# Dealing out the matmuls of two neighbouring TensorE operations in turn, in a fused recurrence and long-convolution kernel

## The chip, the cores and the metric

The kernel runs on one core of one Trainium2 chip. The core's engines work side by side, each on its own queue of instructions: TensorE (PE, matmuls; PEld is its loading of weights), VectorE (DVE), ScalarE (ACT), GpSimd (POOL) and SyncE (SP, which here issues the transfers). The metric is the device time of one execution in microseconds. Before the change the median of three runs is 458.21 us (456.58 to 459.52).

## The reference

Two parts follow each other on x of shape 4 x 6272 x 256. First a gated recurrence along the sequence, then a gated long convolution through the Fourier transform:

```python
sig = 1.0 / (1.0 + np.exp(-f_logit))
f = lower_bound + (1.0 - lower_bound) * sig
for t in range(S):                              # S = 6272
    h = f[:, t] * h + (1.0 - f[:, t]) * x[:, t]
    y[:, t] = h

x1, x2, x3 = split(y @ w_proj)                  # three times 256 columns
conv = irfft(rfft(x2, axis=1) * rfft(filter_fft, axis=0), axis=1)
out = (x1 * conv * x3) @ w_out
```

## The kernel before

The four sequences (batches) are worked through one after the other, and the recurrence of the next batch runs beside the convolution of the current one. The sequence length is 6272 = 128 x 49, and the Fourier transform is done as matmuls with small tables in two steps.

The recurrence (`hgrn`) goes in 13 chunks of 512 positions (the last has 128). For each chunk SP loads x and f_logit, ACT takes the sigmoid (L335), POOL multiplies (`u`, L337). Data arrive with positions on the partitions, and the scan needs channels there, so for each half of the channels PE transposes both tensors into PSUM: this is the **transposing operation** `su` (function `turn`, L344 to L350). It makes 16 transposes of 64 x 128 fp32 values (4 in the last chunk): for the gate (from FL), then for x (from XT), for each of four blocks, for the lower and the upper 64 partitions. ACT or DVE then makes the gate factor from one part of the result (`f`, L362 or L364), and DVE scans with it and the other part (L370).

The convolution of a batch has these operations on PE: `P` (L714) projects x2; `F1` (L727) is the first step of the transform; `mini` (L743) and **`F2`, the DFT over q** (function `mm` in `unit`, L784 to L792) the second; DVE multiplies the result by the filter's spectrum (L813), or ACT copies it (L284) and POOL multiplies (L822). `I2` (L832) is the first step back, ACT copies its result into Th (L284), and **`I1`, the inverse DFT over m** (function `inv` in `phase_o`, L886 to L897) the second. DVE multiplies I1's result by the gates (`y`, L901), `proj` (L913) applies w_out, ACT copies the result out and SP stores it. `x13` (L398) makes the gate projections. F2 is 8 matmuls with 64 rows of weights and 256 columns, in pairs for the lower and upper 64 partitions; I1 is 16 matmuls with 64 rows and 128 columns (4 in the last group), in such pairs too. All three kinds use 64 of the 128 rows at a time.

The order of the work is not found by a scheduler at build time. Every piece of work is recorded with `op`, with its predecessors, and the string `ORDER` holds, for each of the 2429 recorded operations, its number, the engine that does it and the first of its PSUM banks (there are eight; su, F2 and I1 take two). `Plan.emit` goes through this string and calls each operation's function, so the instructions of each engine's queue stand in the order of the string. Waits are put in by the framework where an instruction reads what another engine writes, or writes where another still reads, a PSUM bank too.

Of the kernel before, what the change touches and what calls it, by code (L numbers as in the profile page):

```python
# [24 lines left out]
Q = 49  # L25
# [12 lines left out]
UE = 8  # L38
# [18 lines left out]
def m0_of(r):  # L57
    return (128 * q_of(r) - r) // Q


class Plan:

    ROWS = ("su", "F2", "mini", "I1", "FF2", "last")
    ANY = ()
    ENGINES = ("ACT", "DVE", "PE", "POOL", "SP", "MUL")
# [41 lines left out]
    def emit(self):  # L107
        rows, seen = False, set()
        for i, e, b in self.order():
            o = self.ops[i]  # L110
            assert e in o["cost"] and i not in seen and o["preds"] <= seen
# [4 lines left out]
            if e == "PE" and o["kind"] in self.ANY:  # L116
                args.append(rows)
            elif e == "PE":
                rows = o["kind"] in self.ROWS
            o["fn"](*args)  # L120
        assert len(seen) == len(self.ops)
# [51 lines left out]
    "Z7YbxSbzqeTGb1Tb2Qb4Ab3DeJgb6RZrUaCYb0YZ5Yb5YeUOb8BZsEb7Qb9ob+YaBSaFqaGYaDCaEYeWWaKQeXGeeUaMAeYOefEZ+SaNYegMZ/Ca"
    "Oob/QcBAaPYaLYewgeiWe7gaTSeVAcAQcCocDYaXCejGaHUaUYaVqaWYaIEaYYcETcFRcGDe6geBYcHpcIYcJQcLAcKUcOVcPQcMscNYeoAcQNcR"
    "ocTRcVBepYcSYekOaQSaRCeNgaZUaaEcUQcWocXYcYRcaBcZScbqehYccYcdUceMeyAexgciWcjOezYeqQetSfFgfEgeuCevKerAesIcfUcgEchg"
    "ckWclGcsSctKi6Ui8EeZge8AcnWcoOe9Ye0Qe3UfPgfOgcmgcuSe1AcpWe2Ie4Ee5McvCcqGc2Qc3Ie+ScxUfBWfYgcyMfGAfCGfZgc4Qe/CfDOA"
    "uUc5Ac6gfHYfQAfRYfAKi7Ui/Vi9EdAQfIWfJGdBIczSjBFc7QfKOc8Ic0CfLUfjgfSWfigfMEfVScwgc9QfTGfaAfNMfUOdCUfWCfXKelYfbYdF"
    "Wc+AdDEjAQdGOjCAdKSfcUffQdLKdHWfdEfeMcrgfkAflYfgAdMSfhIc1gdIGfmUfpWfnEfoMfqGfrOdUQdVIdNCdPUdQMgCWgDOfwSfxCgAQgBA"
# [16 lines left out]
def kernel(  # L195
# [10 lines left out]
    nc = tc.nc  # L206
# [7 lines left out]
    iden = konst.tile([128, 128], F32, name="iden")  # L214
# [16 lines left out]
    A = HA[:, A0:A0 + AW].rearrange("m (e r k) -> m e r k", r=2, k=64)  # L231
# [17 lines left out]
    FF2 = [("FF2", u) for u in range(NU)] + ["FF2"]  # L249
# [7 lines left out]
    PS = psp.tile([128, 8, 512], F32, name="PS")  # L257
# [61 lines left out]
    def hgrn(b):  # L319
        for c in range(NCHK):  # L320
            t0 = c * CH
            nb = min(CH, S - t0) // 128
            n = nb * 128
            if b == 0:
                k = c % (NX + len(more))
            else:
                k = count["x"] % NX
                count["x"] += 1
            xt, ft = (more[k - NX] if k >= NX else (XT[:, k], FL[:, k]))
            xt, ft = xt[:, 0:nb], ft[:, 0:nb]  # L330
            for dst, src, t in ((ft, f_logit, ("ft", k)), (xt, x, ("xt", k))):
# [6 lines left out]
                xt, xt, ft, op=AOP.mult), r=[("ft", k)], w=[("xt", k)])  # L338
            for kh in range(2):
                cols = slice(kh * 128, kh * 128 + 128)  # L340

                hn = 64 * nb

                def turn(e, pb, ft=ft, xt=xt, cols=cols, nb=nb, hn=hn):  # L344
                    for src, at in ((ft, (0, 768)), (xt, (512 - hn, 512))):
                        for j in range(nb):
                            for p in range(2):
                                ps = slice(64 * p, 64 * p + 64)
                                nc.tensor.transpose(bank(pb)[:, at[p] + j:at[p] + hn:nb],  # L349
                                                    src[ps, j, cols], iden[ps, ps])  # L350
                su = op("su", {"PE": 0.126 * nb}, turn, r=[("ft", k), ("xt", k), "iden"], w=["qT"], take=2)
                j = count["f"] % 2
# [5 lines left out]
                def gate_f(e, pb, fT=fT, hn=hn, kh=kh):  # L358
# [8 lines left out]
                   r=["om"], w=[("fT", j)], src=su)  # L367
# [406 lines left out]
    def unit(b, u):  # L774
# [9 lines left out]
        def mm(e, xb):  # L784
            for o in range(2):
                ks = slice(32 * o, 32 * o + 32)
                for r in range(2):
                    for e2 in range(2):
                        rows = slice(64 * e2, 64 * e2 + 64)
                        nc.tensor.matmul(  # L790
                            PS[:, xb + e2, :].rearrange("p (i k) -> p i k", k=64)[:, :, ks],
                            FT[rows, o, r, :], A[rows, ka:ka + UE, r, ks],  # L792
                            start=(r == 0), stop=(r == 1))
# [88 lines left out]
    def phase_o(b):  # L882
        for g, r0 in enumerate(range(0, Q, 4)):
            rn = min(4, Q - r0)

            def inv(e, cb, r0=r0, rn=rn):  # L886
                tf = late["Th"][:].rearrange("p c b a g -> p (c b a g)")
                for i in range(rn):
                    r = r0 + i
                    sh = (128 - m0_of(r)) % 128  # L890
                    for rr in range(2):
                        c0 = (rr * Q + r) * 128
                        for p in range(2):
                            ps = slice(64 * p, 64 * p + 64)
                            nc.tensor.matmul(PS[:, cb + p, i * 128:(i + 1) * 128],  # L895
                                             tf[ps, c0:c0 + 128], ID[ps, rr, sh:sh + 128],
                                             start=(rr == 0), stop=(rr == 1))  # L897
# [99 lines left out]
```

## Time and profile before

| | |
|---|---|
| median of 3 runs | 458.21 us (456.58 to 459.52) |
| the profiled execution, from first to last instruction | 455.6 us |
| PE busy | 439.6 us, 96%, 6009 matmuls |
| weight loads (PEld) busy | 348.4 us, 76% |
| DVE busy | 407.4 us, 89% |
| ACT busy | 402.3 us, 88% |
| POOL busy | 308.8 us, 68% |
| transposes of su (L349) | 1568 |
| matmuls of F2 (L790), of I1 (L895) | 512, 784 |

Matmuls are pipelined: each is recorded for longer than the distance between two starts, and their ends are modelled, so a busy PE is not a PE at its peak, and the pace of a block of matmuls is read from the starts. Lower and upper halves of a pair start within a few nanoseconds of each other. A line of the timeline merges neighbouring instructions of one kind: start in us from the span's start, length, engine, line, operation, what it writes and reads, shape, count, and in brackets the idle time ahead of it with what ended it. In a group's line, busy time and mean length of one are followed by the idle time of the engine just ahead of such instructions.

### The profile page before, as it was taken

Reading aid. Unit: us, or ns where it says so; the run is one execution under the profiler, and the core shown is the slowest. Engines: PE = TensorE matmul, PEld = TensorE weight load, DVE = VectorE, ACT = ScalarE, POOL = GpSimd, SP = SyncE. Lnnn points to the kernel's source line nnn. Section 1 sums busy time; section 2 is a strip of 40 time slices with the busy share of each in tenths; the row PEclk is TensorE's granted clock in tenths of the full one; section 3 lists DMA queues with packets and bytes.
Section 4 is the critical chain, followed back from the end, with each engine's and each line's share of the span. In section 5 each row is a group of like instructions: output and inputs, shape, how many; then the busy total and the mean of one; then the engine's idle time right before and its main releaser. Section 6 shows DMA issues by size and latency. Waiting matters only on the chain.

```text
span 455.6 us, 14635 instructions
## 1 busy us (share of the span) xinstructions
PE 439.6 (96%) x6009; PEld 348.4 (76%) x6009; DVE 407.4 (89%) x476; ACT 402.3 (88%) x577; POOL 308.8 (68%) x279
## 2 busy tenths in 40 slices
PE   7899999999999999999999999999999999999998
PEld 5687778677767888777668888777778896776797
DVE  8899997799999996999999977999999976989873
ACT  5899999899999987899989998999989858987563
POOL 8888973878899542788995626899994405696400
PEclk9599999999999999999999999999999999999999
DMA  8999999767898985479776896778759721765186
GB/s 326 387 371 345 378 375 361 279 187 233 299 300 282 340 300 237 169 232 374 253 264 219 285 315 272 237 250 303 261 177 317 301 95 46 248 187 185 47 321 246
DMA packets 44434, 120.74 MB, mean 265 GB/s; under 512 B 4304, under 2 KB 7632, under 8 KB 44368
## 3 DMA queue, kind: packets, MB, share of 16 engines
q1 hardware_dynamic: 44368, 119.82, 74.5%
q8 instruction: 47, 0.77, 0.7%
q14 instruction: 19, 0.16, 0.1%
HBM read 86.12 MB, written 31.98 MB: 259 GB/s over the span
## 4 chain that ended last, share of the span: by engine, by line
PE 72%; DVE 11%; ACT 9%; issue 4%; DMA 3%; POOL 1%; SPq 0%; ACTq 0%; DVEq 0%; POOLq 0%
PE PS L398 17%; PE PS L714 9%; PE PS L832 9%; PE PS L913 8%; PE PS L790 7%; DVE HA L370 7%; PE PS L727 6%; PE PS L349 6%; PE PS L895 4%; ACT fTs L362 2%; DMA X<-in_moe_filter_fft_dram 2%; PE PS L600 2%; ACT HA L284 2%; DVE ys L901 1%; ACT X L284 1%
## 5 line engine op out<-in xcount | busy, mean ns | idle before, releaser
L337 POOL TENSOR_TENSOR XT<-XT,FL 128x1024 f32<-128x1024 f32 (+1 forms) x49 | 109.9, 2247 | 55.7 <-ACT FL L335 38.5
L370 DVE TENSOR_TENSOR_SCAN HA<-fTs,HA,PS 128x512 f16<-128x512 f32 (+1 forms) x96 | 112.7, 1202 | 2.0 <-ACT fTs L362 1.1
L398 PE MATMUL PS<-HA,W 128*128 128x490 f16 (+1 forms) x416 | 100.2, 367 | 0.3 <-ACT Th L284 0.2
L822 POOL TENSOR_TENSOR PP<-HA,Hu 98x1008 f16<-98x1008 f16 x42 | 88.0, 2106 | 5.6 <-ACT HA L284 2.6
L284 ACT CAST HA<-PS 128x1024 f16<-128x1024 f32 (+1 forms) x101 | 81.2, 831 | 3.3 <-POOL PP L822 0.8
L901 DVE TENSOR_TENSOR ys<-PS,zt 128x1024 fp32r<-128x1024 f32 (+1 forms) x52 | 58.3, 1151 | 14.0 <-PE PS L895 10.3
L813 DVE TENSOR_TENSOR PP<-PS,Hu 98x1008 f16<-98x1008 f32 x54 | 63.6, 1199 | 1.5 <-PE PS L790 0.7
L362 ACT ACTIVATE fTs<-PS,nomc 128x512 f32<-128x512 f32 (+1 forms) x90 | 59.5, 680 | 4.5 <-PE PS L349 4.2
L398 PEld LDWEIGHTS <-W 128*128 128x128 f16 x416 | 35.3, 97 | 30.2 <-issue 2.9
L428 POOL TENSOR_TENSOR zt<-XS 128x490 f16<-128x490 f32 (+1 forms) x26 | 31.8, 1223 | 39.0 <-DVE ys L901 27.4
L913 PE MATMUL PS<-Wo,ys 128*128 128x256 f32 x392 | 57.5, 293 | 0.4 <-DVE ys L901 0.3
L286 ACT ACTIVATE XS<-PS 128x490 f32<-128x490 f32 (+1 forms) x88 | 51.0, 590 | 6.8 <-DVE zt L419 2.6
L832 PEld LDWEIGHTS <-PP 98*128 98x128 f16 x1024 | 49.2, 98 | 10.1 <-POOL PP L795 1.3
L284 ACT CAST Th<-PS 128x784 f16<-128x784 f32 x63 | 52.0, 828 | 3.4 <-PE PS L832 2.7
L913 PEld LDWEIGHTS PS<-Wo,ys 128*128 128x128 f32 x392 | 49.6, 188 | 4.5 <-DVE ys L901 1.2
L832 PE MATMUL PS<-VA,PP 98*128 98x98 f16 x512 | 52.1, 207 | 0.2 <-POOL PP L795 0.2
L832 PE MATMUL PS<-VB,PP 98*128 98x98 f16 x512 | 51.8, 207 | 0.0
L419 DVE TENSOR_TENSOR zt<-PS,XS 128x490 f16<-128x490 f32 (+1 forms) x78 | 49.2, 648 | 2.7 <-ACT XS L286 0.8
L335 ACT ACTIVATE FL<-FL 128x1024 f32<-128x1024 f32 (+1 forms) x49 | 49.8, 1022 | 0.6 <-DMA FL<-in_f_logit_dram 0.6
L714 PE MATMUL PS<-W,HA 128*128 128x256 f16 x392 | 44.6, 273 | 1.1 <-ACT X L284 1.1
L714 PEld LDWEIGHTS <-HA 128*128 128x128 f16 x392 | 42.9, 142 | 2.0 <-issue 1.3
L349 PE MATMUL PS<-iden,FL 64*128 64x64 f32 x736 | 41.7, 229 | 2.6 <-ACT PP L286 0.6
(119 smaller groups left out, 778.7 us busy)
## 6 DMA issues: line engine op xcount, KB each, us to landing
FL<-in_f_logit_dram SPq DMA_DIRECT2D x45, 512.0 KB, 5.3
XT<-in_x_dram SPq DMA_DIRECT2D x45, 512.0 KB, 6.2
Hu<-H SPq DMA_DIRECT2D x39, 512.0 KB, 4.6
out_dram<-osb SPq DMA_DIRECT2D x24, 512.0 KB, 4.6
out_dram<-PP SPq DMA_DIRECT2D x16, 512.0 KB, 4.8
Hl<-H SPq DMA_DIRECT2D x13, 512.0 KB, 4.7
X<-in_moe_filter_fft_dram SPq DMA_DIRECT2D x9, 512.0 KB, 7.0
out_dram<-HA SPq DMA_DIRECT2D x8, 512.0 KB, 5.7
```

Source lines behind the costliest of these rows:

```text
L284: nc.scalar.copy(dst, src)
L337: op("u", {"POOL": 0.1 + 0.553 * nb}, lambda e, xt=xt, ft=ft: nc.gpsimd.tensor_tensor(xt, xt, ft, op=AOP.mult), r=[("ft", k)], w=[("xt", k)])
L349: nc.tensor.transpose(bank(pb)[:, at[p] + j:at[p] + hn:nb], src[ps, j, cols], iden[ps, ps])
L362: nc.scalar.activation(fT, sT, AF.Identity, scale=by, bias=1.0)
L370: nc.vector.tensor_tensor_scan(h, fT, bank(pb)[:, 512 - hn:512 + hn], init, op0=AOP.mult, op1=AOP.add),
L398: nc.tensor.matmul(PS[:, p, 0:n], W13[:, kh, js], HA[:, HB[kh] + t0:HB[kh] + t0 + n], start=(kh == 0), stop=(kh == 1))
L714: nc.tensor.matmul(pp[:, r - r0, :], column(HB[kh], q_of(r)), W2[:, kh, :], start=(kh == 0), stop=(kh == 1))
L813: nc.vector.tensor_tensor(pr, px.unsqueeze(1).broadcast_to([TB, 2, UE, 63]), hh(), op=AOP.mult)
L822: nc.gpsimd.tensor_tensor(pr, spec[:, o, :, 1:64].unsqueeze(1).broadcast_to([TB, 2, UE, 63]), hh(), op=AOP.mult)
L832: nc.tensor.matmul(PS[:, ib + o, pr * TB:(pr + 1) * TB], PP[:TB, k, o, n, 2 * pr:2 * pr + 2, :], v[:TB], start=(n == 0), stop=(n == 1))
L901: nc.vector.tensor_tensor(late["ys"][:, yk, :, 0:rn * 128], PS[:, cb:cb + 2, 0:rn * 128], late["zt"][:].rearrange("p k r m -> p k (r m)") ...
L913: nc.tensor.matmul(po[:, i, :], late["ys"][:, yk, kh, i * 128:(i + 1) * 128], Wo[:, kh, :], start=(kh == 0), stop=(kh == 1))
```

## The change

Forty times, two operations that stand next to each other in PE's order, one of them su and the other F2 (19 times) or I1 (21 times), are marked in the order string with a new engine name, `JOIN`, on the first of the two. Their functions now give back lists of small pieces instead of issuing everything: a piece is one pair of matmuls for the lower and upper 64 partitions. For a marked pair, `alternate` issues one piece of the first, one of the second, and so on. su gives 8 pieces (2 in the last chunk), I1 gives 8. F2 gives 4 pieces of 256 columns when it stands alone, and in a marked pair 8 pieces of 128 columns, with the weights loaded for each. In the string the second operation of a pair is moved up next to the first, past entries of other engines only; the order of operations on each engine stays as it was, apart from the alternation itself.

```diff
-    ENGINES = ("ACT", "DVE", "PE", "POOL", "SP", "MUL")
+    PIECES = ("su", "F2", "I1")
+    ENGINES = ("ACT", "DVE", "PE", "POOL", "SP", "MUL", "JOIN")
...
+            if e == "JOIN":
+                joined = o["fn"](e, b)
+                continue
             args = [e]
             if o["take"] or o["src"] is not None:
                 args.append(b)
...
+            if joined is not None:
+                assert e == "PE" and o["kind"] in self.PIECES
+                self.alternate(joined, o["fn"]("JOIN", b))
+                joined = None
+            elif o["kind"] in self.PIECES:
+                for piece in o["fn"](*args):
+                    piece()
+            else:
+                o["fn"](*args)
...
+    def alternate(a, b):
+
+        for k in range(max(len(a), len(b))):
+            for pieces in (a, b):
+                if k < len(pieces):
+                    pieces[k]()
...
-                    for src, at in ((ft, (0, 768)), (xt, (512 - hn, 512))):
-                        for j in range(nb):
-                            for p in range(2):
-                                ps = slice(64 * p, 64 * p + 64)
-                                nc.tensor.transpose(bank(pb)[:, at[p] + j:at[p] + hn:nb],
-                                                    src[ps, j, cols], iden[ps, ps])
+                    def piece(src, at, j):
+                        for p in range(2):
+                            ps = slice(64 * p, 64 * p + 64)
+                            nc.tensor.transpose(bank(pb)[:, at[p] + j:at[p] + hn:nb],
+                                                src[ps, j, cols], iden[ps, ps])
+                    return [lambda src=src, at=at, j=j: piece(src, at, j)
+                            for src, at in ((ft, (0, 768)), (xt, (512 - hn, 512))) for j in range(nb)]
...
+            n = UE // 2 if e == "JOIN" else UE
+
+            def piece(o, i, r):
                 ks = slice(32 * o, 32 * o + 32)
-                for r in range(2):
-                    for e2 in range(2):
-                        rows = slice(64 * e2, 64 * e2 + 64)
-                        nc.tensor.matmul(
-                            PS[:, xb + e2, :].rearrange("p (i k) -> p i k", k=64)[:, :, ks],
-                            FT[rows, o, r, :], A[rows, ka:ka + UE, r, ks],
-                            start=(r == 0), stop=(r == 1))
+                for e2 in range(2):
+                    rows = slice(64 * e2, 64 * e2 + 64)
+                    nc.tensor.matmul(
+                        PS[:, xb + e2, :].rearrange("p (i k) -> p i k", k=64)[:, i:i + n, ks],
+                        FT[rows, o, r, :], A[rows, ka + i:ka + i + n, r, ks],
+                        start=(r == 0), stop=(r == 1))
+            return [lambda o=o, i=i, r=r: piece(o, i, r)
+                    for o in range(2) for i in range(0, UE, n) for r in range(2)]
...
+                return [lambda i=i, rr=rr: piece(i, rr) for i in range(rn) for rr in range(2)]
```

More of the change, by code (lines that the diff above doesn't have):

```diff
@@ L61 @@
 class Plan:
-    ROWS = ("su", "F2", "mini", "I1", "FF2", "last")
-    ANY = ()
-    ENGINES = ("ACT", "DVE", "PE", "POOL", "SP", "MUL")
+    PIECES = ("su", "F2", "I1")
+    ENGINES = ("ACT", "DVE", "PE", "POOL", "SP", "MUL", "JOIN")
     def __init__(self):
@@ L107, in emit @@
     def emit(self):
-        rows, seen = False, set()
+        seen, joined = set(), None
         for i, e, b in self.order():
             o = self.ops[i]
-            assert e in o["cost"] and i not in seen and o["preds"] <= seen
+            assert e in o["cost"] or e == "JOIN" and "PE" in o["cost"]
+            assert i not in seen and o["preds"] <= seen
             seen.add(i)
+            if e == "JOIN":
+                joined = o["fn"](e, b)
+                continue
             args = [e]
@@ L115, in emit @@
                 args.append(b)
[L116 to L121, printed above, removed]
+            if joined is not None:
[7 more added lines that the diff above has]
+                o["fn"](*args)
+        assert len(seen) == len(self.ops) and joined is None
+    @staticmethod
+    def alternate(a, b):
[3 more added lines that the diff above has]
+                    pieces[k]()
 ORDER = (
@@ L144 @@
-    "dgJQqNeANogK3XK4SK0BK1GNpgK2YK5HK6qJVUJRYK7YNfYJXENUQNVAK8WNWIK+GNYTNygNzgMrgNZDK9SK/CLAYLBXLCWJJQNaLLGSJZsLDHLE"
+    "H8YH6YHuEIHSIICIFWIGGH9oH+YKTYKUUKWMKVVKZQKXFKYYH2SH3CKbIIUgIJWIM0MkQIKOIOsINYIQEIRYMlAIdgIVSImgIZCMmIH/WIXqIAGI"
+    "YYIWYIPYMoUMpEMqMNEgKaTKcDIvQIwAIaYISWIfYI5gKJYIeyMwQIgKIhYITGIiqIjYIbUMxAMyIKeSIcEKdYNFgKgCM02InUM1GIzSIrsIsYIp"
+    "EIqYNQgIoYJCgI0CIkQIlAM2OKfUKjVKkSKlFKhsNGANHYI6QKmqKnYI8oI+oI/YI9YNRgIxWIyGI1UItSI2EM8WJLgMngIuCI3UI4MI7YJDwNAS"
+    "JFoM9GJGYNcgJEYJHAJIYM+ONBCJAUKoRKpQNSANTYKqBNCKNIWJBENJGKroKsYKtRKvBJNYNM0JMSNNENKOJOCNOMJUgKuQKyRKzWJPYKwoKxYN"
@@ L145 @@
+    "dgJQqNeANogK3XK4SK0BK1GNpgK2YK5HK6qJV0NUQJRYK7YNfYJXENVAK8WNWIK+GNYTNygNzgMrgNZDK9SK/CLAYLBXLCWJJQNaLLGSJZsLDHLE"
     "uLFYNqALIKJKAJaYJSTJTDLHXNgQNkVN8gNhANlFLJvLKYNbgNiILLUNrYLMSLQTLNEJYYLRXLOqNmNLSDLVUKiYLTHN9gLXEM/gJWYNsQNtALWS"
-    "NvTLYqLZYN0ANwDLUYLaVLPYNuINxLJbWJcGOHgN1YLbSR8QR9RLfWLcFNnYLdqLeYLgOR+AR/BN+ALkULlMN2SN/YOGgN3CN4KN5QNXYOQgN6AN"
-    "7ILhWLiGLmUNDALuSLvKNPYLpWLnELqOOIAOAQOBAOCILjgORgODUObgOagOJYLwSOEELxCLrWLsGLtgOFML4QL5ILogOKSOSANLgLzWONUOlgOk"
-    "gL0OOOEOLCL6QL7AL1WL9QL8gL2GOcAMzAOPMOTYOMKL+IMCUOUWOXSOYCMDMVAgOZKU/gL/QOVGOWOMAAOdYMEUMFEMHSMIKOeQOfAOgIOhUVLg"
@@ L149 @@
-    "OiEM3YVMgOjMOmASBWSCXSEHSDGMJSMKCOnYOoQOpIOrWOsGOqIMBgNjAOtOVXgLygMMUMRSVYgVNAMNMMSKL3gVBAO2QPAWO8UO3IMLgO9EPBGM"
+    "NvTLYqLZYN0ANwDLUYLaVLPYNuINxLJbWJcGOHgN1YLbSR8QR9RLfWLcFNnYLdqLeYLgOR+AR/BN+ALk0N2SLlMN/YOGgN3CN4KN5QNXYOQgN6AN"
+    "7ILhWLiGLmUNDALuSLvKNPYLp2OAQLnELqOOIAOBAOCILjgORgODUObgOagOJYLwSOEELxCLrWLsGLtgOFML4wOKSL5ILogOSANLgLz2ONUOlgOk"
+    "gL0OOOEOLCL6QL7AL1WL9QL8gL2GOcAMzAOPMOTYOMKL+IMC0OUWOXSOYCMDMVAgOZKU/gL/QOVGOWOMAAOdYMEUMFEMHyOeQMIKOfAOgIOhUVLg"
+    "OiEM3YVMgOjMOmASBWSCXSEHSDGMJSMKCOnYOoQOpIOr2MMUOsGOqIMBgNjAOtOVXgLygMRSVYgVNAMNMMSKL3gVBAO2QPAWO8UO3IMLgO9EPBGM"
@@ L152 @@
     "SQVSRQQFgPksPnYSOpQOgPlYSSFSToPfYPgSPhCPjYPvYP0UP1ESVXSXHPsuPtYQXgP2QP3IPoSPpCP9UQBsPrYP4WSUYP5GVOYSWQSaRScBP/sQ"
-    "qgQAYPwSP6WP7OQHYP+YQCYPxCSbRSdBSYoQGUQIEQJYSeYQKsQzgVDSVECQgQQhAVFKQLYQDWQQYQEGQPUQRsQYQQaAQTsQUYQ8gQkSQlCQMWQc"
+    "qgQAYPwSP6WP7OQHYP+YQCYPxCSbRSdBSYoQG0VDSQIEQJYSeYQKsQzgVECQgQQhAVFKQLYQDWQQYQEGQPUQRsQYQQaAQTsQUYQ8gQkSQlCQMWQc"
     "oQbYRFgQdYQZYSfQQNGSgUQiSQSYShAQjCSkVQmWMagQnGSmNQVQQWAQrSSisSjYVHUVjgQtqQoWQpOQvCQwYSZYVkgSlQSnoSpRQeSVIEVJMQuY"
-    "SrBQfCQsYQ0WQ4GQ2uQ3YQ5YRYgVPQVQAVTSVwgVvgRhgQxUVRIVUCVVKQ1YSqXSuWQyESsHStYRQUQ+YSwGRSQRREQ9WQ/uRBuRGSRTARKCQ6UR"
+    "SrBQfCQsYQ02VPQQ4GQ2uQ3YQ5YRYgVQAVTSVwgVvgRhgQxUVRIVUCVVKQ1YSqXSuWQyESsHStYRQUQ+YSwGRSQRREQ9WQ/uRBuRGSRTARKCQ6UR"
@@ L156 @@
     "HYROQRCYQ7ERIqSoYVGYRPARLYRJYSvWSzTS1DSxuRAYRqgRDUS0XS2vVlAVmYS3YMdQMeAMfgRZSRbqRdqRcYRUWVbQREES4SSPYSyYVKgRVGRW"
-    "URXMRaYVcAVxAVdIRMWRjYRNGS5TS7DVfUV7gV8gRrWVnQS6CVyYS8YReYRvGVWYRzgVgMVoAVhMVpIVrSWHgWIgRtGS9XS+UVegVqgS/HTAsVsC"
-    "VtKRfVRsYRgFRwYTCXTDQTHRTIWTEHTFoTGYTJBTKuRiURuYRksV9AVzSV0CRmEV3QWSgWRgV1KTMWTLYTOGRnYV+YTNXTPvTRUTTETSVTUtTWWV"
-    "4AV5IRxSTQYTXXTbURyCTcVTgSTYGThTTdETZvWJAWKYTetTiKRlYRoQR1YTjrTkYRpAR0UR4ER2sV/WR3YWDQWbgWcgTBYWAGWBOWEATlSTmTTn"
+    "URXMRaYVcAVxAVdIRMWRjYRNGS5TS7DVf0RrWV7gV8gVnQS6CVyYS8YReYRvGVWYRzgVgMVoAVhMVpIVrSWHgWIgRtGS9XS+UVegVqgS/HTAsVsC"
@@ L160 @@
+    "VtKRfVRsYRgFRwYTCXTDQTHRTIWTEHTFoTGYTJBTKuRi0VzSRuYRksV9AV0CRmEV3QWSgWRgV1KTMWTLYTOGRnYV+YTNXTPvTRUTTETSVTUtTWWV"
+    "4AV5IRxSTQYTXXTbURyCTcVTgSTYGThTTdETZvWJAWKYTetTiKRlYRoQR1YTjrTkYRpAR00V/WR4ER2sR3YWDQWbgWcgTBYWAGWBOWEATlSTmTTn"
     "CTorTpYTfYR5YTqUTsETrVTttTvSTwUWLWTuYTxCWFITyETzYR6SWMGWNOR7CT0UT1VT2ET3tTVYTaYT5QT6RT7AT8pT9YT+SabQSKYWTAT4YT/K"
-    "adAWUYUDUUEMWOWViYWlgUIQWPGWQOUASUJIWmgWdAUBCUCgUFUUGEUNWUOOWeYWVSWYQWvgWWCWXKUKUWZAWfWWaIULEWwgUSSUTKWiUW5gWgGW"
-    "6gUPQWhOWnAWjEWkMUQAUHgUUSUVCWxAUXWUYOUcQUdIWoYWpUWqEWrMWsSXDgXEgWtCWuKWyYW7AW8YUZWAgQUaGUhQUiIWzUW2WV2AWCYW3GW4"
@@ L163 @@
-    "OUMgdfgW0EW1MUeSUfCUjQUmWUnOUkAW9SW+CW/KXAQXBAXCIXFAXGYacUagVaiFUbgV6AdqgaeEdegUoWXHSXICXJKXKUd2gXLEXMMVSAUrQUsI"
+    "adAWUYUD0WOWUEMViYWlgUIQWPGWQOUASUJIWmgWdAUBCUCgUFUUGEUN2WVSUOOWeYWYQWvgWWCWXKUKUWZAWf2USSWaIULEWwgUTKWiUW5gWgGW"
+    "6gUPQWhOWnAWjEWkMUQAUHgUUSUVCWxAUXWUYOUcQUdIWoYWpUWqEWrMWsSXDgXEgWtCWuKWyYW7AW8YUZWAgQUaGUhwWzUUiIW2WV2AWCYW3GW4"
+    "OUMgdfgW0EW1MUeSUfCUjQUm2W9SUnOUkAW+CW/KXAQXBAXCIXFAXGYacUagVaiFUbgV6AdqgaeEdegUoWXHSXICXJKXK0UrQd2gXLEXMMVSAUsI"
     "d3gUpGUwSUxKVuYWGYXTUXlWXmGXUMXNQURgXOAXXWUWgXYGXVSd4AXfQXgAXRUXSMUtWUqgUuOXhQdgAXiIXWCXPUXQMXZSd5YdsAdrgdhYXjWX"
@@ L165 @@
     "aCXbQXkGXdSXcAUggXeCU6UU1WU2OUyQU7MUzAUvgafYXnSXpWXqGXrUUlgXsEU0gahQalRanBXoKajoXtSXuCXxWXzuakYX0YX1uamQaqRaoAas"
-    "BdtYU3UXvSU4EX2YU5gapYXwKX6YXyYX5QX9oX+YdiWYRSarUatsavVX7AX8YX3QYCYYbgdjGdkOYSCaxFYBSYFqX4AYDCdmUeCgeDgYEYdnEdoM"
+    "BdtYU3UXvSU4EX2YU5gapYXwKX6YXyYX5wdiWX9oX+YYRSarUatsavVX7AX8YX3QYCYYbgdjGdkOYSCaxFYBydmUYFqX4AYDCeCgeDgYEYdnEdoM"
     "auYYJWawQYLGX/RYMYYKYYNuYOYa0Ta2LYkgYABa1Wa3Ga4YYTUYGYayoYVRduWYUEdvOa5TazYY2gYWBa7DYXUdwOYYEa6QYtga8Aa+RbAJdlYa"
-    "9YYHSYICYZUYaMYdYYcWYgGYhYYeuYlQYpAYPSYqYYmYdxYa/UYfYYQCbDRYnoYoYbEVYuSeEAYwCbFJdyWdzGd6QbGtePgbISbBsbHYbJUbNVYy"
+    "9YYHSYICYZUYaMYdYYcWYgGYhYYeuYlQYpAYPSYqYYmYdxYa/UYfYYQCbDRYnoYoYbEVYuydyWeEAYwCbFJdzGd6QbGtePgbISbBsbHYbJUbNVYy"
@@ L173 @@
[L173 to L177, printed above, removed]
@@ L178 @@
-    "Wc+AdDEjAQdGOjCAdKSfcUffQdLKdHWfdEfeMcrgfkAflYfgAdMSfhIc1gdIGfmUfpWfnEfoMfqGfrOdUQdVIdNCdPUdQMgCWgDOfwSfxCgAQgBA"
+    "EZnoaSgZoYZxSZyCZqYeKWemgeLGbCYbnRbrQbppbqYbtIbsUeRYecAZiSZmYblYbwVbyFeMOengZjCAlQbusedYZ4weSWbvYZ8oZ9YZ1UZ2MZ6A"
+    "Z7YbxSbzqeTGb1Tb2Qb4Ab3DeJgb6RZrUaCYb0YZ5Yb5YeUOb8BZsEb7Qb9ob+YaByeWWaFqaGYaDCaEYaKweeUeXGaMAeYOefEZ+SaNYegMZ/Ca"
+    "Oob/QcBAaPYaLYewgei2aTSe7geVAcAQcCocDYaXCejGaHUaUYaVqaWYaIEaYYcETcFRcGDe6geBYcHpcIYcJQcLAcKUcOVcPQcMscNYeoAcQNcR"
+    "ocTRcVBepYcSYekOaQSaRCeNgaZUaaEcUQcWocXYcYRcaBcZScbqehYccYcdUceMeyAexgci2eqQcjOezYetSfFgfEgeuCevKerAesIcfUcgEchg"
@@ L179 @@
+    "ckWclGcsSctKi6Ui8EeZge8Acn2e0QcoOe9Ye3UfPgfOgcmgcuSe1AcpWe2Ie4Ee5McvCcqGc2we+Sc3Icx0fBWfYgcyMfGAfCGfZgc4Qe/CfDOA"
+    "uUc5Ac6gfHYfQAfRYfAKi7Ui/Vi9EdAwfIWfJGdBIczSjBFc7wfLUfKOc8Ic0CfjgfSWfigfMEfVScwgc9QfTGfaAfNMfUOdCUfWCfXKelYfbYdF"
+    "Wc+AdDEjAQdGOjCAdKyfcUffQdLKdHWfdEfeMcrgfkAflYfgAdMSfhIc1gdIGfmUfp2dUQfnEfoMfqGfrOdVIdNCdPUdQMgCWgDOfwSfxCgAQgBA"
     "f2Uf3Mf0Sf1Kf8Qf9IfsUftEf6Wf7GfuSfvCf4Qf5IfyUfzEgESgFCf+Wf/GdRQc/gdSAdZSdaKgGUgHEdJggKWgLOgISgJCgMQgNAjDYgQUi+Yj"
@@ L887, in inv, with piece @@
                 tf = late["Th"][:].rearrange("p c b a g -> p (c b a g)")
[L888 to L897, printed above, removed]
+                def piece(i, rr):
+                    sh = (128 - m0_of(r0 + i)) % 128
+                    c0 = (rr * Q + r0 + i) * 128
+                    for p in range(2):
+                        ps = slice(64 * p, 64 * p + 64)
+                        nc.tensor.matmul(PS[:, cb + p, i * 128:(i + 1) * 128],
+                                         tf[ps, c0:c0 + 128], ID[ps, rr, sh:sh + 128],
+                                         start=(rr == 0), stop=(rr == 1))
+                return [lambda i=i, rr=rr: piece(i, rr) for i in range(rn) for rr in range(2)]
             i1 = op("I1", {"PE": 0.115 * rn}, inv, r=[("Th", u) for u in range(NU)] + ["ID"], take=2)
```

8 lines of the change are left out of this document (1 added, 7 removed).

## The prediction

> **What bounds the kernel now.** First the page: engine shares (busy us, share, instructions) and the chain that ended last.
>
> ```profile
> span 455.6 us, 14635 instructions
> ...
> PE 439.6 (96%) x6009; PEld 348.4 (76%) x6009; DVE 407.4 (89%) x476; ACT 402.3 (88%) x577; POOL 308.8 (68%) x279
> ...
> PE 72%; DVE 11%; ACT 9%; issue 4%; DMA 3%; POOL 1%; SPq 0%; ACTq 0%; DVEq 0%; POOLq 0%
> PE PS L398 17%; PE PS L714 9%; PE PS L832 9%; PE PS L913 8%; PE PS L790 7%; DVE HA L370 7%; PE PS L727 6%; PE PS L349 6%; PE PS L895 4%; ACT fTs L362 2%; DMA X<-in_moe_filter_fft_dram 2%; PE PS L600 2%; ACT HA L284 2%; DVE ys L901 1%; ACT X L284 1%
> ```
>
> TensorE (PE) holds 72% of the chain, DVE and ACT together 20%. The lines of the change, L349 (transposes), L790 (DFT) and L895 (inverse DFT), are 17% of it. Next come busy times by stretch; all 40 joined pairs lie between 107.9 and 365.0 us.
>
> ```profile
> core 0: us, PE busy (x) PEld busy (x) DVE busy (x) ACT busy (x) POOL busy (x), PEclk, DMA share, GB/s
> 107.90:365.00 257.10, 251.90 (x3790) 199.39 (x3792) 241.50 (x262) 240.42 (x349) 188.28 (x142) 1.00 0.78 271
> 285.00:335.00 50.00, 50.00 (x743) 36.40 (x742) 48.91 (x61) 48.79 (x76) 47.87 (x41) 1.00 0.76 261
> ```
>
> PE idles 257.1 - 251.9 = 5.2 us there. In 285 to 335 us PE, DVE and ACT are full at once: a delay on any of the three has little to hide behind. The clock is 1.00 throughout, so it plays no part.
>
> **The change, part by part.** In before, an operation's matmuls stand in one block: 16 transposes (8 pieces of two, one for each half of the rows), then 16 inverse-DFT matmuls (8 pieces) or 8 DFT matmuls of 256 columns. After, 40 neighbouring blocks a and b are dealt out a, b, a, b. In the listing of the built program DVE, ACT, POOL and SP keep their order and instructions, no queue is passed and no DMA moves; PE keeps the order of its operations. Of the pairs 21 hold an inverse DFT and 19 a DFT; each of these 19 is split into 16 matmuls of 128 columns, so PE gets 19 x 8 = 152 more matmuls and as many weight loads. Three pairs hold a short transposing operation of 2 pieces, so there are 37 x 8 + 3 x 2 = 302 transposing pieces.
>
> *PE's own work.* Durations of one, by shape:
>
> ```profile
> L398 PE MATMUL PS<-HA,W 128*128 128x490 f16 x384 | 94.1, 370 | 0.3 <-ACT Th L284 0.2
> L349 PE MATMUL PS<-iden,XT 64*128 64x64 f32 x736 | 39.6, 223 | 0.6 <-POOL XT L337 0.6
> L790 PE MATMUL PS<-HA,FT 64*128 64x256 f16 x512 | 37.9, 271 | 0.2
> L895 PE MATMUL PS<-ID,Th 64*128 64x128 f16 x784 | 28.7, 216 | 1.0 <-DVE HA L370 0.5 <-ACT X L284 0.3 <-ACT PP L286 0.2
> L349 PEld LDWEIGHTS PS<-iden,FL 64*128 64x128 f32 x736 | 32.1, 138 | 13.7 <-DVE HA L370 2.6 <-ACT afs L284 1.3 <-ACT PP L286 1.3
> L895 PEld LDWEIGHTS <-Th 64*128 64x128 f16 x784 | 23.6, 94 | 7.6 <-issue 3.5 <-ACT Th L284 0.9 <-ACT XS L286 0.3
> ```
>
> These overlap, so the pace is read from starts. The timeline of a pair with an inverse DFT and of one with a DFT, both without a wait between a and b (start, length, engine, line, count):
>
> ```profile
> 240.69 0.37 PE L398 MATMUL PS<-HA,W 128*128 128x490 f16 x1
> 240.99 0.62 PE L895 MATMUL PS<-ID,Th 64*128 64x128 f16 x16
> 241.45 0.41 PE L349 MATMUL PS<-iden,FL 64*128 64x64 f32 x8
> 241.71 0.42 PE L349 MATMUL PS<-iden,XT 64*128 64x64 f32 x8
> 241.96 0.61 PE L895 MATMUL PS<-ID,Th 64*128 64x128 f16 x16
> ...
> 299.48 0.61 PE L790 MATMUL PS<-HA,FT 64*128 64x256 f16 x8
> 299.93 0.41 PE L349 MATMUL PS<-iden,FL 64*128 64x64 f32 x8
> 300.17 0.41 PE L349 MATMUL PS<-iden,XT 64*128 64x64 f32 x8
> 300.42 0.35 PE L349 MATMUL PS<-iden,FL 64*128 64x64 f32 x6
> ```
>
> Inverse DFT: 241.45 - 240.99 = 0.46 us for 8 pieces, 57 ns each. Transposes: 0.25 us for 4 pieces, 62 ns each, and it stays 0.25 (241.71 to 241.96) when the next thing is no transpose but an inverse DFT, whose load is short (94 against 138 ns). So a transposing piece holds its place for about 62 ns whoever follows: the time lies in the matmul itself, or at least as much there as in the load. Its 223 ns say the same: columns cost (370 - 216)/(490 - 128) = 0.43 ns each, 64 of them would make 189, and 223 are 34 more. The other seam, inverse DFT to transpose, stands inside the 0.46: a full 57. Dealt out, a pair of pieces then takes 57 + 62 as before. A DFT block is 0.45 us for 4 pieces of 256 columns, or 8 halves of 56: nothing again. I take **0** for PE's work (bounds: -35 ns for each transposing piece if its excess over 64 x 0.43 = 27 ns could hide, which is rival B; and a price for switching, rival C).
>
> The Trainium skill's TensorE: Matmul & The Clock Gate, section Weight-path perf modes, has loads of 128 weights fast unless they are FP32, and its section What happens when you issue a matmul has a load pulled ahead under a running matmul. By these and its N/2.4 + 2.5 ns a transposing piece would take an estimated 29 ns once its load hides, and the change would save about 10 us of PE work; the 0.25 us seam speaks against it.
>
> *Waits of b, now inside a.* This is the cost I expect. An operation writes two PSUM banks and waits at its first matmul until their last reader is done. PE takes the matmuls in the program's order, so after the change b's first piece, second in the row, holds back 7/8 of a.
>
> ```profile
> 121.87 0.89 ACT L284 CAST Th<-PS 128x784 f16<-128x784 f32 x1
> ...
> 122.20 0.72 PE L790 MATMUL PS<-HA,FT 64*128 64x256 f16 x8
> ...
> 122.82 0.46 PE L349 MATMUL PS<-iden,FL 64*128 64x64 f32 x8
> 123.07 1.20 DVE L813 TENSOR_TENSOR PP<-PS,Hu 98x1008 f16<-98x1008 f32 x1
> 123.11 0.42 PE L349 MATMUL PS<-iden,XT 64*128 64x64 f32 x8
> 123.16 0.67 ACT L284 CAST HA<-PS 98x512 f16<-98x512 f32 x1
> ```
>
> ACT's Th copy frees b's banks at 121.87 + 0.89 = 122.76. In before the DFT block fills that time, and the transposes start at 122.82 having lost 0.06 us. After, PE does one DFT piece at 122.20, then stands from 122.26 to 122.81: 0.55 us idle, and the pair ends 0.49 us later than now. I read all 40 pairs so (start of a, end of the last reader of b's banks, remaining pieces at the paces above; where the x half of the transposes comes late, L337 at half way). First and last:
>
> ```profile
> 107.39 0.66 DVE L291 TENSOR_SCALAR XS<-PS 128x490 f32<-128x490 f32 x1
> 107.91 0.77 PE L790 MATMUL PS<-HA,FT 64*128 64x256 f16 x8
> ...
> 364.39 0.28 PE L349 MATMUL PS<-iden,FL 64*128 64x64 f32 x2
> 364.89 0.80 PE L895 MATMUL PS<-ID,Th 64*128 64x128 f16 x18 [0.16 <-DVE HA L370]
> ```
>
> The first frees at 108.05 and loses 0.12 us, the last loses 0.11. Nine of the 40 lose nothing (240.99 is one), the worst 0.59; together **7.7 us** of new PE idle time.
>
> *Consumers of a.* a's last piece comes just ahead of b's last, so whoever reads a is released later by b's length (about 0.45 us) plus the stall: over the 40 pairs 27.6 us, 19.9 of it beyond the PE delay itself. In the fence above DVE L813 (123.07) and ACT L284 (123.16) take the DFT's result at once; released 1.1 us later, ACT has only L362 of the transposes next, which ends up late too. Waits of this kind exist already:
>
> ```profile
> DVE ys L901 <- PE PS L895: 10.3, 8, 2.7
> ACT fTs L362 <- PE PS L349: 4.2, 11, 1.3
> ```
>
> (total us, times, longest). b's consumers gain nothing: b does not end sooner.
>
> *Sum.* How much reaches the end? I weigh by the chain's shares: PE delay 7.7 x 0.72 = 5.5; consumers' delay 19.9 x 0.20 = 4.0; together 9.5, of which I take 9, as the nine pairs without a stall show that slack exists. Bounds: 0 (the 5.2 us of PE idle time and unread slack take all) and 27.6 (all of it lands). The profiled span is 455.6; the median of the runs lies 2.6 above. 458.2 + 9 = **467 us**.
>
> **Rivals.**
>
> *A, slack takes it.* Engines that come late at one pair catch up before the next; pairs are 257/40 = 6.4 us apart and the mean delay is 0.7. For it: POOL and DMA work is unaffected, and 5.2 us of PE idle time is there. Against: the full stretch 285 to 335, with 8 pairs in it. It gives 0 to 4 us: 458 to 462.5.
>
> *B, the transposes' loads hide (the side that is not slower).* If 35 of the 62 ns are the FP32 load, and the DFT's matmul covers it, PE saves 302 x 35 ns = 10.6 us. Place: between a DFT piece and the next transposing piece, where loads could run 57 ns ahead. For it: the 138 against 94 ns of load. Against: the 0.25 us seam. Net: 467 - 10.6 x 0.72 = 459.4. It decides from 9/0.72/302 = 41 ns a piece: above that the kernel is not slower than before. If stalls are slight too (A and B), about 451.
>
> *C, switching costs.* Going from 128-row to 64-row matmuls costs now: 240.69 to 240.99 is 0.30 us where 490 columns at 0.43 take 0.21. Should a transpose and a DFT matmul (both 64-row) charge a tenth of these 90 ns at each of some 14 new switches, 40 x 14 x 9 ns x 0.72 = 3.6 us more: 471; with a fifth, 474 and beyond. Against: neither seam at 241.45 nor at 241.96 shows any.
>
> **How the numbers follow.** Forecast 0.55 (463 to 473); A 0.15; B 0.20, of which 0.08 ends below 453.6; C 0.10. The measurement tells about 1% (4.6 us) from no change. Faster by over 1%: 0.08. Within: A and the rest of B, 0.27. Slower: 0.65. Low end 456 takes in A and most of B; the high end is 7.7 whole plus 0.4 of 19.9, so 15.7 on 458.2: 474.
>
> **What would show it.** In the profile after: L349, L790 and L895 interleave in the 40 places; starts of successive pieces stay 57 and 62 ns apart (B: they shrink to about 57 + 30; C: they grow). In the place that is now 122.20, PE idles some 0.5 us between the first DFT piece and the first transposes, ended by ACT L284. PE idle time before L349 and L895 grows by some 5 to 8 us in sum, the waits of ACT L284, DVE L813 and L901 for L790 and L895 grow by several us, and PE's share of the span falls. PE matmuls count 6161. Wrong I am if the pace inside pairs shrinks well below 119 ns for two pieces, or if idle time grows but the span doesn't.

## The result, and the profile after

The changed kernel takes 470.97 us (median of 4 runs, 469.57 to 472.74), the kernel before 457.4 us in the same comparison: ratio 1.0293, 95% interval 1.0257 to 1.0329, or 11.8 to 15.0 us slower. The forecast was 467 us (456 to 474), so the direction was right, and the loss of 13.4 us is half again as large as the 9 expected.

In the listing of the changed kernel lines have moved: the transposes stand on L363 (before L349), the DFT on L807 (L790), the inverse DFT on L913 (L895), ACT's copies on L299 (L284), its gate factor on L378 (L362), DVE's scan on L386 (L370), its product with the spectrum on L832 (L813). From the page of the changed kernel, engine shares and the chain that ended last:

```profile
span 469.0 us, 14940 instructions
...
PE 443.0 (94%) x6161; PEld 350.1 (75%) x6161; DVE 409.9 (87%) x476; ACT 404.1 (86%) x577; POOL 308.7 (66%) x279
...
PE 64%; ACT 13%; DVE 13%; issue 5%; DMA 3%; POOL 1%; SPq 0%; ACTq 0%; DVEq 0%; POOLq 0%
```

The engines do the same work (DVE 409.9 against 407.4 us, ACT 404.1 against 402.3; PE 443.0 against 439.6 with 152 more matmuls, whose recorded times overlap), and each of them has a smaller share of a longer span: they wait more. The chain's share on PE fell from 72 to 64%, that on ACT and DVE rose from 20 to 26%. By stretch, the one with the pairs:

```profile
core 0: us, PE busy (x) PEld busy (x) DVE busy (x) ACT busy (x) POOL busy (x), PEclk, DMA share, GB/s
108.00:376.00 268.00, 255.34 (x3941) 201.23 (x3939) 243.01 (x262) 241.31 (x347) 188.10 (x142) 1.00 0.76 261
295.00:345.00 50.00, 48.29 (x783) 35.98 (x782) 45.83 (x58) 45.93 (x70) 45.32 (x39) 1.00 0.72 241
```

PE now idles 268.0 - 255.3 = 12.7 us there (5.2 before). The stretch in which PE, DVE and ACT were all full (50.00, 48.91 and 48.79 of 50 us) has holes on all three. The pace of the matmuls is unchanged. This is the timeline of a pair without a wait, which alternates all the way:

```profile
360.98 0.22 PE L913 MATMUL PS<-ID,Th 64*128 64x128 f16 x2
361.04 0.23 PE L363 MATMUL PS<-iden,FL 64*128 64x64 f32 x2
361.10 0.22 PE L913 MATMUL PS<-ID,Th 64*128 64x128 f16 x2
361.15 0.23 PE L363 MATMUL PS<-iden,FL 64*128 64x64 f32 x2
361.22 0.22 PE L913 MATMUL PS<-ID,Th 64*128 64x128 f16 x2
361.27 0.23 PE L363 MATMUL PS<-iden,FL 64*128 64x64 f32 x2
361.33 0.22 PE L913 MATMUL PS<-ID,Th 64*128 64x128 f16 x2
```

From one inverse DFT piece to the next are 361.33 - 360.98 = 0.35 us for three of each kind: 117 ns for two pieces, where blocks took 57 + 62 = 119. A pair with a DFT, from 240.72 to 241.43 us in this trace, gives 0.71 us for six of each kind, 118 ns. And this is the place whose counterpart in before the prediction showed at 122.20, all engines:

```profile
124.68 0.87 ACT L299 CAST Th<-PS 128x784 f16<-128x784 f32 x1
...
124.99 0.29 PE L807 MATMUL PS<-HA,FT 64*128 64x128 f16 x2
...
125.61 0.28 PE L363 MATMUL PS<-iden,FL 64*128 64x64 f32 x2 [0.33 <-ACT Th L299]
...
126.49 0.23 PE L363 MATMUL PS<-iden,XT 64*128 64x64 f32 x2
...
126.74 1.21 DVE L832 TENSOR_TENSOR PP<-PS,Hu 98x1008 f16<-98x1008 f32 x1 [0.81 <-POOL PP L814]
126.77 0.58 ACT L299 CAST HA<-PS 98x512 f16<-98x512 f32 x1 [0.62 <-ACT fTs L378]
```

One DFT piece starts at 124.99; the first transposes stand until ACT's Th copy is done (124.68 + 0.87 = 125.55) and start at 125.61. So PE starts nothing for 0.55 us, as worked out; the pair takes 0.39 us longer than in before, where 0.49 was worked out. The two readers of the DFT start 1.75 and 1.78 us after it (126.74, 126.77), where it was 0.87 and 0.96 (123.07 and 123.16 after 122.20), and both engines stand idle for it, 0.81 and 0.62 us. The brackets name POOL and ACT, but in the trace the queues of DVE and ACT stand on a wait for PE until 126.70 and 126.74; POOL (126.08 + 0.53 = 126.61) and ACT's L378 (126.15) were done before. The two costs of the forecast are both to be seen here.

### The profile page after: what moved, and what is told of

It is laid out like the page before. It is cut to its first block, busy times and chain, and to the rows that moved or that the text cites. A ratio compares the mean times of both kernels' runs of the same rounds, so it can differ in the third digit from the quotient of the medians.

```text
span 469.0 us, 14940 instructions
## 1 busy us (share of the span) xinstructions
PE 443.0 (94%) x6161; PEld 350.1 (75%) x6161; DVE 409.9 (87%) x476; ACT 404.1 (86%) x577; POOL 308.7 (66%) x279
## 4 chain that ended last, share of the span: by engine, by line
PE 64%; ACT 13%; DVE 13%; issue 5%; DMA 3%; POOL 1%; SPq 0%; ACTq 0%; DVEq 0%; POOLq 0%
PE PS L414 15%; PE PS L730 9%; PE PS L932 8%; PE PS L851 7%; PE PS L363 7%; DVE HA L386 6%; PE PS L807 6%; PE PS L743 6%; PE PS L913 3%; ACT fTs L378 3%; DVE ys L920 3%; ACT HA L299 2%; DMA X<-in_moe_filter_fft_dram 2%; ACT Th L299 2%; PE PS L671 2%
## 5 line engine op out<-in xcount | busy, mean ns | idle before, releaser
L386 DVE TENSOR_TENSOR_SCAN HA<-fTs,HA,PS 128x512 f16<-128x512 f32 (+1 forms) x96 | 112.7, 1201 | 4.2 <-ACT fTs L378 3.4
L299 ACT CAST HA<-PS 128x1024 f16<-128x1024 f32 (+1 forms) x101 | 80.6, 824 | 9.0 <-PE PS L363 3.2
L832 DVE TENSOR_TENSOR PP<-PS,Hu 98x1008 f16<-98x1008 f32 x54 | 63.7, 1199 | 5.9 <-PE PS L363 1.6
L378 ACT ACTIVATE fTs<-PS,nomc 128x512 f32<-128x512 f32 (+1 forms) x90 | 58.4, 668 | 8.7 <-PE PS L363 6.2
L363 PE MATMUL PS<-iden,FL 64*128 64x64 f32 x736 | 49.8, 231 | 7.0 <-DVE HA L386 2.1
L299 ACT CAST Th<-PS 128x784 f16<-128x784 f32 x63 | 51.8, 827 | 3.9 <-PE PS L851 3.0
L363 PEld LDWEIGHTS PS<-iden,FL 64*128 64x128 f32 x736 | 38.0, 138 | 19.6 <-DVE HA L386 4.7
L807 PE MATMUL PS<-HA,FT 64*128 64x256 f16 (+1 forms) x664 | 47.6, 246 | 1.4 <-ACT Th L299 0.9
```

The source lines that it names most:

```text
L299: nc.scalar.copy(dst, src)
L363: nc.tensor.transpose(bank(pb)[:, at[p] + j:at[p] + hn:nb], src[ps, j, cols], iden[ps, ps])
L378: nc.scalar.activation(fT, sT, AF.Identity, scale=by, bias=1.0)
L386: nc.vector.tensor_tensor_scan(h, fT, bank(pb)[:, 512 - hn:512 + hn], init, op0=AOP.mult, op1=AOP.add),
L807: nc.tensor.matmul(PS[:, xb + e2, :].rearrange("p (i k) -> p i k", k=64)[:, i:i + n, ks], FT[rows, o, r, :], A[rows, ka + i:ka + i + n, r, ...
L832: nc.vector.tensor_tensor(pr, px.unsqueeze(1).broadcast_to([TB, 2, UE, 63]), hh(), op=AOP.mult)
```

## The experiments

Theory: (1) b's wait for its PSUM banks now stands in the middle of a, and PE idles; (2) a's readers are released late; PE's own work is the same. Rivals: the extra matmuls or the switching between kinds cost time, so that every pair costs alike; or one of (1) and (2) is the whole of it. All edits below are against the changed kernel. Added lines shown alone stand in place of the four lines that the first edit takes out of `alternate`, but for the run in which b starts after half of a, which keeps them; `first` and `kind` are the kinds of a and of b, handed over as a third argument. Differences are against the kernel before, run on the same chip, and worked out as (ratio - 1) x 457.4 to 458.1 us. The ratio on record is not the quotient of the two medians and differs from it by up to 0.3%: in the first run below the median is 457.34 us and that of before 457.74. A delay is said to land as far as it lengthens the whole kernel. The lateness of a is how much longer than in before a takes from its first to its last matmul; it delays a's readers. All latenesses below are sums over the pairs.

**Halves without alternation.**

```diff
-        for k in range(max(len(a), len(b))):
-            for pieces in (a, b):
-                if k < len(pieces):
-                    pieces[k]()
+        for piece in a + b:
+            piece()
```

> The 40 pairs stay in blocks, one operation after the other; only the 19 DFTs of the pairs are cut into halves of 128 columns. Theory (the loss is b's wait standing inside a, and a's readers released late): no loss, 0 to +0.5 us against before (19 x 8 more matmuls at 2 to 3 ns). Rival 'more PE work' (the 152 extra matmuls and loads cost): +3 us or more of the 13.4.

Measured: 457.34 us, ratio 1.0017 (0.9993 to 1.0041), +0.8 us (-0.3 to +1.9). The 152 extra matmuls are not where the 13.4 us are. All runs below have these halves in the pairs that they keep marked, as the changed kernel has.

**Eleven pairs, and the other 29.**

```diff
+    FREE = (844, 760, 755, 775, 1140, 1283, 1293, 1582, 1674, 1831, 1856)
...
+            if e == "JOIN" and i not in self.FREE:
+                e = "PE"
             if e == "JOIN":
```

> Only the 11 pairs alternate in which b's banks were free before a's second piece in the trace of before; the other 29 run as in before. Theory: hardly a wait is added, only 11 x 0.44 us of later release of a's readers, of which a fifth lands: about +1 us. Rival 'every alternating pair costs alike' (switching, or late readers landing whole): 11/40 of 13.4 = +3.7 us.

With `i in self.FREE` the other 29 alternate:

> Only the other 29 pairs alternate, those in which b had to wait for its banks. Theory: nearly all of the loss, +11 to +13 us. Rival 'every pair costs alike': 29/40 of 13.4 = +9.7 us.

Measured: eleven pairs 459.45 us, ratio 1.0047 (1.002 to 1.0074), +2.2 us (0.9 to 3.4); the 29 others 470.64 us, ratio 1.0263 (1.0225 to 1.0302), +12.0 us (10.3 to 13.8). Alike per pair would be 3.7 and 9.7, outside both intervals. The loss is 0.20 us for each of the eleven and 0.41 for each of the others, which have the waits; but the lateness of a is larger there too, 0.78 us a pair against 0.47, so this run does not tell the two apart. And 2.2 is twice what I gave the eleven, a first sign, within the interval, that late readers were priced too low.

**The wait alone.** b's first piece stands second, then a is finished, then b:

```diff
-        for k in range(max(len(a), len(b))):
-            for pieces in (a, b):
-                if k < len(pieces):
-                    pieces[k]()
+        for piece in a[:1] + b[:1] + a[1:] + b[1:]:
+            piece()
```

> All 40 pairs, but dealt out only once: first piece of a, first piece of b, then the rest of a as a block, then the rest of b. b's wait for its banks stands in the same place as in after, but a is finished one block earlier (0.4 us) than in after. Theory by the forecast's weights: the PE waits remain, 7.7 to 8.8 us of pair time, and with what they delay +8 to +10 us. Rival 'late readers are the main loss': +4 us or less.

**The late reader alone.** Only a's last piece is put off:

```diff
+        for piece in a[:-1] + b[:-1] + a[-1:] + b[-1:]:
+            piece()
```

> All 40 pairs, blocks as in before, but the last piece of a is put off until just before the last piece of b. b's wait stands behind seven pieces of a as in before, so PE waits no longer; a's readers are released 0.4 us late, 40 x 0.43 = 17 us in sum. Theory by the forecast's weights: a fifth lands, +2 to +4 us. Rival 'late readers are the main loss': +9 us or more.

Measured: wait alone 463.35 us, ratio 1.0137 (1.0102 to 1.0173), +6.3 us (4.7 to 7.9); late reader alone 465.51 us, ratio 1.0182 (1.0149 to 1.0215), +8.3 us (6.8 to 9.8). Neither reading of what the main loss is holds by itself. The first came out below the 8 to 10 us that I expected, the second at more than double. The sum, 14.6, is the 13.4 of the whole within the intervals, but the two runs do not split it cleanly: the wait holds a back as well, so the lateness of a is 13.5 us with the wait alone, 23.0 with the late reader alone, and 28.6 in the changed kernel, less than the two together.

Where does the late reader cost? The same place in the run with late readers alone (its listing is two lines shorter: transposes L361, DFT L805, scan L384):

```profile
123.62 0.62 PE L805 MATMUL PS<-HA,FT 64*128 64x128 f16 x14
...
124.24 0.46 PE L361 MATMUL PS<-iden,FL 64*128 64x64 f32 x8
124.54 0.35 PE L361 MATMUL PS<-iden,XT 64*128 64x64 f32 x6
...
124.73 0.22 PE L805 MATMUL PS<-HA,FT 64*128 64x128 f16 x2
...
125.04 1.21 DVE L830 TENSOR_TENSOR PP<-PS,Hu 98x1008 f16<-98x1008 f32 x1 [0.47 <-issue]
125.06 0.58 ACT L297 CAST HA<-PS 98x512 f16<-98x512 f32 x1 [0.28 <-ACT fTs L376]
```

PE goes from the 14 DFT matmuls to the transposes as in before (0.62 us from start to start, 0.62 there: 122.20 to 122.82), yet the readers start 1.42 and 1.44 us after the DFT began instead of 0.87 and 0.96, and DVE idles 0.47, ACT 0.28 us. They are full engines (in 107.9 to 135 us of before DVE is busy for 26.3 and ACT for 26.85 of 27.1 us), and PE later waits for what they free: here are idle times ahead of the transposes and their weight loads, by what ended them, in before and then in this run (us, times).

```profile
  DVE HA L370: 2.6, 8
```

```profile
  DVE HA L384: 5.3, 15
```

The waits for DVE's scan double; with the halves alone they are 2.4 us (8 times) and with the added PE work below 2.5 (8). So part of the lateness comes back to PE as such waits. They are a sign and not the sum: they grew by 2.7 of the 8.3 us, and the run below in which b starts after half of a has the same 5.3 (15) and loses 2.9. I summed, over the 40 places, the time from a's first to b's last matmul less the same in before: 8.8 us in the changed kernel, 7.3 with the wait alone, 2.1 with the late reader alone. Their spans are 13.4, 6.6 and 8.3 us longer than the 455.6 of before. The run with the wait loses about what its pairs lengthen, the run with the late reader loses mostly outside the pairs (6.2 of its 8.3).

**Does it follow the dose?** First b starting only after half of a, alternating from there:

```diff
+        n = len(a) // 2
+        for piece in a[:n]:
+            piece()
+        a = a[n:]
         for k in range(max(len(a), len(b))):
```

> All 40 pairs alternate, but b starts only after half of a. Waits of b shorter than about 0.3 us are covered again, longer ones lose half as much, and a's readers are late by half a block (0.2 us). Theory: about half of the loss, +5 to +7 us. A rival with a fixed price for each switch between the two kinds would keep half of the switches, and also give half; so this run only tells whether loss follows dose.

Measured: 460.95 us, ratio 1.0063 (1.0036 to 1.009), +2.9 us (1.6 to 4.1). That is under a quarter of the loss with half of the switches kept, so a price for each switch cannot be the main loss; and it is below my theory's +5 to +7. I took it for a hint that the first 0.2 us of lateness is slack, and tried that alone:

```diff
+        n = len(b) // 2
+        for piece in a[:-1] + b[:n] + a[-1:] + b[n:]:
+            piece()
```

> All 40 pairs, blocks, the last piece of a put off by half of b only (0.2 us instead of 0.4). Theory 'the first 0.2 us is slack and only what goes beyond lands' (as the run with a lag of half a block hints, +2.9 us): +1 to +2.5 us. Rival 'a fixed share lands': half of +8.3, +4 us.

Measured: 461.29 us, ratio 1.0089 (1.0066 to 1.0113), +4.1 us (3.0 to 5.2). That is half of 8.3 and more than the +1 to +2.5 of the slack theory. But the trace shows that the dose was not half: the lateness of a is 14.4 us, 0.36 us a pair, against 23.0. An even share of it would be 5.2 us, just at the end of the interval. Counting only what goes beyond 0.2 us in each pair, it is 6.4 us here, 15.0 in the run with late readers alone and 4.4 in the run with the lag (lateness 11.6); at 8.3 us for 15.0 that gives an estimated 3.5 and 2.4 us, inside both intervals. So slack of about 0.2 us is not ruled out, and the two runs, whose intervals overlap, do not decide it.

This run also serves to price the wait. With the wait alone the lateness of a is about the same (13.5 us), the pairs take 7.3 us longer instead of 0.9, and the loss is 6.3 instead of 4.1 us. So some 2 us of the 6.3 are left for the wait itself, and the intervals allow from nothing to 5.

**Which reader?** The late reader in the pairs led by one kind alone:

```diff
+        if first == "F2":
+            order = a[:-1] + b[:-1] + a[-1:] + b[-1:]
+        else:
+            order = a + b
+        for piece in order:
+            piece()
```

> As the run that only puts off the last piece of a, but in the 15 pairs alone whose first operation is the DFT over q. Its readers are two, a product on DVE and a copy on ACT, in the stretches where PE, DVE and ACT are full at once. Theory 'a late reader costs where its engine is full': 15 x 0.58 = 8.7 us of lateness, about half lands: +4 to +5 us. Theory 'lateness lands evenly': 8.7/23.0 of +8.3 = +3.1 us.

> The same in the 17 pairs alone whose first operation is the inverse DFT over m; its one reader is the product y on DVE, in stretches where DVE already waits for PE at times. Theory 'a late reader costs where its engine is full': 8.9 us of lateness, a quarter lands: +1 to +2.5 us. Theory 'lateness lands evenly': 8.9/23.0 of +8.3 = +3.2 us.

> The last piece of a put off until just before the last piece of b in the 8 pairs alone whose first operation is the transposing one (readers: gate factor on ACT or DVE, then the scan on DVE, each chunk's scan following the last one's). By difference from the runs with all pairs (+8.3), with those led by the DFT (+2.9) and by the inverse DFT (+1.5): +3.9 us if the three kinds add up, about half a microsecond a pair. If lateness lands evenly: 5.4/23.0 of +8.3 = +1.9 us, and then the kinds reinforce each other.

| led by | pairs | lateness in sum, us | ratio (interval) | loss, us | lands |
|---|---|---|---|---|---|
| DFT | 15 | 8.6 | 1.0064 (1.0042 to 1.0086) | 2.9 | 34% |
| inverse DFT | 17 | 8.5 | 1.0032 (1.0002 to 1.0062) | 1.5 | 17% |
| transposes | 8 | 4.8 | 1.0064 (1.0032 to 1.0096) | 2.9 | 61% |
| all, in one run | 40 | 23.0 | 1.0182 (1.0149 to 1.0215) | 8.3 | 36% |

Lateness is that of the pairs of the row's kind in that run; 1.0 us of the DFT's comes with the halves alone. The kinds add up within the intervals (7.3 against 8.3). As measured the transposes' readers are the dearest per microsecond and the inverse DFT's the cheapest, but the intervals (1.9 to 3.9, 0.1 to 2.8 and 1.5 to 4.4 us) overlap. At an even share of 36% the rows would lose 3.1, 3.1 and 1.7 us: only the inverse DFT lies outside that. The theory of full engines has its +1 to +2.5 us for the inverse DFT, but for the DFT it gave +4 to +5, above the interval. So it is half borne out and not shown.

**A delay of PE by itself.** Blocks, and one transposing piece done four times more in each place:

```diff
+        if kind == "su":
+            b = b + 4 * b[-1:]
+        else:
+            a = 4 * a[:1] + a
+        for piece in a + b:
+            piece()
```

> Blocks as in before (DFTs of the pairs in halves), but in each of the 40 places one piece of the transposes is done four times more, 4 x 62 ns = 0.25 us of PE time, 9.9 us in sum; the result is the same. It prices a delay of PE by itself at these places. Theory with the forecast's weight: 0.72 lands, +7 us. Rival 'a PE delay lands whole': +10 us, which would explain why after lost 13.4 and not 9. Rival 'slack takes it': +3 us or less.

Measured: 463.09 us, ratio 1.011 (1.0067 to 1.0152), +5.0 us (3.1 to 7.0): half of the 9.9 us lands (the pairs take 8.6 us longer in this trace). The forecast's 0.72 (+7) is just at the edge of the interval, the rival that all lands (+10) is out. Its chain:

```profile
PE 73%; DVE 9%; ACT 9%; issue 4%; POOL 2%; DMA 2%; SPq 0%; DVEq 0%; ACTq 0%; POOLq 0%
```

The share on PE (73%) is no forecast of how much of a delay of PE lands.

## Why the prediction was right, and where it was off

*PE's work unchanged: right.* Two pieces take 117 ns alternating and 119 in blocks; halving alone costs 0.8 us with an interval that holds zero. The seam of 0.25 us already told that a transposing piece keeps its place in front of an inverse DFT's piece too. Rival B, by which the transposes' loads would hide, would have shown 57 + 30 = 87 ns for two pieces. The prediction's estimate from the Trainium skill's TensorE: Matmul & The Clock Gate (a load pulled ahead, section What happens when you issue a matmul, and 29 ns for 64 columns, section Back-to-back issue gap) would give 57 + 29 = 86; the trace, with 117, does not agree.

*Rival C, switching: out.* The same 117 ns, and the run with half of the switches loses under a quarter.

*Waits of b inside a: right in mechanism, and nearly in size.* 7.7 us were worked out by reading the trace of before, the pairs took 8.8 longer, and PE starts nothing for 0.55 us in the place shown. PE's idle time ahead of the transposes and the inverse DFT grew from 4.2 to 9.7 us, within the 5 to 8 us of growth forecast.

*Lateness of a's readers: right in its sum, its weight was wrong.* 27.6 us were worked out, 28.6 found. **The mis-sized term is the weight of 0.20**, the chain's share on DVE and ACT, under "Sum" (19.9 x 0.20 = 4.0 us). With the late reader alone 36% of 23.0 us landed; 0.36 on the 19.9 is 7.2 us, and with the 5.5 for the waits the sum is 12.7, inside the measured 11.8 to 15.0. This is worked out afterwards, and loosely: less what its pairs lengthen, 6.2 of 20.9 us landed, 30%, and the sum would be 11.4, just below. The share of a chain tells where one chain ran in one execution. It does not tell what becomes of a delay on engines that are 98% busy in 285 to 335 us: the chain moved over to DVE and ACT (20% to 26%).

*The weight of 0.72 on PE's waits* gave 5.5 us, and the wait alone cost 6.3 (4.7 to 7.9). That the two are near is luck as far as these runs show: the 6.3 contain late readers, and a bare delay of PE landed by half only. An estimate from two runs: let a microsecond by which the pairs lengthen land with one weight and a microsecond of lateness with another. The bare delay (8.6 and 3.0 us, loss 5.0) and the late reader alone (2.1 and 23.0, loss 8.3) then give 0.47 and 0.32, and the changed kernel (8.8 and 28.6) should lose 4.1 + 9.2 = 13.3 us. That would put two thirds of the loss on late readers. But the same weights give 4.7 us for the run with the lag, above its 1.6 to 4.1, so how the loss splits stays open.

*Rival A, slack takes it,* ended at 462.5 us and is out. Slack does show in part: two thirds of the lateness and half of the bare delay did not land.

The forecast was therefore right in its two costs and in their sums, and too low because the late readers were weighed too lightly; its weight for the waits is not borne out.

## What to carry to other kernels

Before two blocks of matmuls are interleaved, look in the trace at two things for each pair: when the second block's banks come free after the first block's start, and how soon after the first block its readers begin. Both had their cover from the block order, and interleaving takes both away: the second one's wait moves into the first, and the first one's result comes as late as the second's. Against these costs interleaving needs a pace of the mix that is better than that of the blocks. Here it was the same (117 and 119 ns), and one seam between two blocks in the old trace had already shown that.

## What the runs showed that I had not expected

A late result can cost as much as added work on the matmul engine: putting off one piece of the first operation, so that its result came 0.58 us later on average in 40 places (23.0 us in sum), cost 8.3 us (6.8 to 9.8), with the pairs only 2.1 us longer and no work added but the halves. In the same places 9.9 us of useless transposes cost 5.0 us (3.1 to 7.0). In a kernel whose three engines are all nearly full, the order in which results come out of PE mattered as well as PE's own time.
